# Batch 1's q and k by token blocks, a ring of six buffers and DMA transposes, in a sliding-window attention and MLP kernel

## The chip, the cores and the metric

The kernel runs on one core of a Trainium2 chip. The metric is the device time of one execution in microseconds (us). Before the change it is 224.65 us, the median of three runs (224.03 to 225.09). Engine names in the profile: PE is TensorE's matmuls, PEld its weight loads, DVE VectorE, ACT ScalarE, POOL GpSimd, SP SyncE, which only issues DMAs here. An ending q (SPq) marks an engine's queue of instructions. Runs are marked fast or slow by their own spread; ratios use fast runs alone.

## The reference, cut to what matters

```python
# q, k, v: (4, 8, 768, 64); n_sink 4, window 128; w_ch1 (512, 2048), w_ch2 (2048, 512)
keep = is_sink | ((rel >= 0) & (rel < 128))           # rel = query position - key position
scores = where(keep, q @ k.T / 8, -1e9)
a = exp(scores - max); a = a / sum(a)
x = (a @ v) as (batch, token, 512)
out = x + relu(layernorm(x) * g_ln @ w_ch1) @ w_ch2
```

The work is cut into 24 row blocks of 128 tokens, six in each of the four batches. Row blocks 6 to 11 are batch 1, 12 to 17 batch 2. Attention of one batch runs on TensorE between the MLP's products of earlier ones ("up" is the product with w1, "down" that with w2). The four sink tokens' scores are a product of their own, for queries 256 to 767.

## The kernel before

A list scheduler in Python walks all operations with estimated costs when the program is built, and so fixes the order in which each engine gets its instructions. In the traces each engine works through its own list in that order. This includes GpSimd and SyncE, which issue the DMAs: a load whose buffer isn't free holds up what stands behind it on that engine (at 86.05 us in the changed kernel's trace a load of q had waited 2.71 us for a transpose, and the six loads of v behind it were issued from 88.37).

```python
JOINED = (1, 3)
qkn = tile_pool(name="qkn", bufs=4)       # one buffer holds q or k of a whole batch
CHUNKS = {0: 2, 1: 1}                     # batches transposed on TensorE; the others by DMA
...
# masks of the attention weights: whichever engine the scheduler finds free
o = op({"POOL": 1.28, "DVE": 0.69}, window, [o, masks_done], key, (), [eb])
...
# batches 2 and 3: a load of 128 tokens, then a DMA transpose of it
def prep(b, x, r, lo, key):
    def go(_):
        nc.sync.dma_start_transpose(kb.t[:, x, :, 128 * r:128 * (r + 1)], qb.t[:, H * D * r:H * D * (r + 1)])
    o = op({"SP": 1.25}, go, [lo], key, alloc, [kb, qb])
...
for c in range(3):
    load_w(2, c, -440 + c)
for x in range(2):
    load_runs(1, 0, x, 0, H, 3.85, -436 + x)      # batch 1: q, then k, 768 KB each
load_w(2, 3, -434)
for r in range(RB):
    load_v(1, r, -430 + r)
load_first_v(1, -424)                              # the sink tokens' v
...
if b == 1:
    for hp in range(HP):
        prep_runs(1, 0, hp, k0 - 12 + 3 * hp)      # TensorE transposes
if b == 2:
    for r in range(RB):
        for x in range(2):
            load_qk(b, x, r, k0 - 60 + r)
    for r in range(RB):
        load_v(b, r, k0 - 50 + r, [prepped[(b, 3, 1)]])
```

The softmax here doesn't subtract the row's maximum and nothing guards it: scores larger than these inputs give would overflow.

## Time and profile before

| | before |
|---|---|
| median of the runs | 224.65 us |
| span of the profiled run | 222.8 us |
| TensorE busy | 215.7 us, 97% |
| share of TensorE in the chain that ended last | 89% |
| packets' time of the loads from GpSimd (q0), of the transposes and stores from SyncE (q1) | 71.6% and 24.8% of 16 engines' span |

TensorE is the bound: it has no idle of over 0.3 us between the start-up and the end. The DMA engines are full for the first half (nine tenths or more in slices 2 to 21 of the 40). The lines are quoted in the prediction. They are from GpSimd's timeline of the kernel before (start, duration, instruction, and in brackets the idle time before it with what ended it): the mask of batch 0's row block 5, and batch 2's six loads of v, issued as one block from 73.50 us.

```profile
33.09 1.09 POOL L642 TENSOR_SCALAR_AFFINE_SELECT e<-e 128x1024 bf16<-128x1024 bf16 x1 [1.11 <-ACT e L630]
...
73.50 5.36 POOL L418 DMA_DIRECT2D vn<-in_v_dram  x6
```

### The profile page before, as it was taken

To read this page: it belongs to the slowest core of one execution; us is meant where nothing else is said; L and a number is where in the kernel's file an instruction comes from. 1 tells how busy PE (TensorE), PEld (TensorE's weight loads), DVE (VectorE), ACT (ScalarE), POOL (GpSimd) and SP (SyncE) were. 2 spreads that over 40 slices of the span, in tenths; PEclk is the share of its full clock that TensorE was granted. 3 is DMA by queue.
4 is the path that set the end of the run, shared out by engine and by line. 5 is a ranking of instruction groups with operands and counts; after the bars stand their busy time and mean duration, and the time that the engine had idled before them with its cause. 6 is when DMAs were issued, how large, how long until landed. Compare 5 with 4: busy or idle time off the path is not lost.

```text
span 222.8 us, 4495 instructions
## 1 busy us (share of the span) xinstructions
PE 215.7 (97%) x1795; PEld 124.3 (56%) x1816; DVE 115.8 (52%) x246; ACT 111.1 (50%) x157; POOL 92.9 (42%) x129
## 2 busy tenths in 40 slices
PE   8999999999999999999999999999999999999994
PEld 7555888975465544455455445444454554444852
DVE  5447867036998898756763574570017660021011
ACT  3489785676761358861237753066603166400620
POOL 8996776449854986888500320120004020000000
PEclk9999999999999999999999999999999999999999
DMA  7999999999999999999993102311011220012102
GB/s 169 160 192 197 191 206 204 205 160 124 144 150 149 222 205 188 142 172 182 154 238 94 23 3 71 98 70 24 1 44 53 71 79 18 0 51 90 50 0 94
DMA packets 88582, 26.11 MB, mean 117 GB/s; under 512 B 78193, under 2 KB 85617, under 8 KB 88562
## 3 DMA queue, kind: packets, MB, share of 16 engines
q0 software_dynamic: 62656, 13.64, 71.6%
q1 hardware_dynamic: 25362, 11.81, 24.8%
q10 hardware_dynamic: 544, 0.39, 0.5%
q8 instruction: 14, 0.23, 0.4%
q14 instruction: 6, 0.05, 0.1%
HBM read 28.05 MB, written 6.29 MB: 154 GB/s over the span
## 4 chain that ended last, share of the span: by engine, by line
PE 89%; DVE 7%; issue 2%; ACT 1%; DVEq 0%; ACTq 0%
PE single L860 36%; PE single L820 35%; PE wide L612 4%; PE single L245 3%; PE single L697 2%; DVE st L749 2%; DVE xt L743 2%; DVE xn L757 2%; PE single L700 2%; PE wide L484 1%; PE wide L608 1%; PE single L680 1%; PE single L796 1%; PE single L484 1%; PE single L560 1%
## 5 line engine op out<-in xcount | busy, mean ns | idle before, releaser
L820 PE MATMUL single<-xnt,w1s 128*128 128x256 bf16 (+1 forms) x506 | 86.8, 325 | 0.3
L820 PEld LDWEIGHTS <-w1s 128*128 128x128 bf16 x512 | 48.8, 98 | 33.8 <-issue 2.1
L630 ACT ACTIVATE e<-wide 128x1024 bf16<-128x1024 f32 x44 | 43.8, 1022 | 47.6 <-PE wide L612 47.5
L860 PE MATMUL single<-w2s,h1t 128*128 128x512 bf16 x247 | 55.6, 379 | 1.0 <-issue 0.8
L873 DVE SCALAR_TENSOR_TENSOR ot<-single,rs,xt 128x512 f32<-128x512 f32 (+2 forms) x25 | 18.2, 728 | 55.5 <-PE single L860 55.0
L829 ACT ACTIVATE h1t<-single 128x512 bf16<-128x512 f32 x59 | 35.2, 597 | 21.3 <-PE single L820 19.8
L860 PEld LDWEIGHTS <-h1t 128*128 128x128 bf16 x256 | 24.6, 98 | 29.9 <-issue 0.9
L860 PE MATMUL single<-w2s,h1n 128*128 128x512 bf16 (+2 forms) x138 | 29.0, 355 | 0.5 <-issue 0.3
L642 POOL TENSOR_SCALAR_AFFINE_SELECT e<-e 128x512 bf16<-128x512 bf16 (+1 forms) x13 | 9.3, 713 | 47.5 <-ACT e L630 47.3
L829 ACT ACTIVATE h1n<-single 128x512 bf16<-128x512 f32 x30 | 17.9, 597 | 22.2 <-PE single L820 22.0
L418 POOL DMA_DIRECT2D vn<-in_v_dram x24 | 21.6, 910 | 0.3 <-DMA qkn<-in_k_dram 0.3
L757 DVE SCALAR_TENSOR_TENSOR xn<-xt,mv,gb 128x512 bf16<-128x512 bf16 x24 | 19.5, 814 | 0.9 <-DVE mv L752 0.3
L860 PEld LDWEIGHTS <-h1n 128*128 128x128 bf16 x144 | 12.7, 98 | 12.9 <-issue 1.1
L769 POOL TENSOR_SCALAR ve<-mv 128x2 f32<-128x2 f32 (+1 forms) x8 | 4.6, 570 | 29.3 <-DVE mv L752 29.1
L749 DVE BATCH_NORM_STATS2 st<-xt 128x6 f32<-128x512 bf16 x24 | 16.5, 688 | 0.3
L736 DVE RECIPROCAL rc<-single 128x4 f32<-128x4 f32 x34 | 6.0, 176 | 18.7 <-PE single L680 14.1
L737 DVE TENSOR_TENSOR xt<-single,rc 128x256 bf16<-128x256 f32 x34 | 14.4, 424 | 1.2
L697 PEld LDWEIGHTS <-e 128*128 128x128 bf16 x192 | 13.1, 98 | 2.5 <-issue 0.2
L612 PE MATMUL wide<-qkt 64*128 64x256 bf16 (+1 forms) x192 | 14.4, 262 | 0.0
L640 DVE TENSOR_TENSOR e<-e,mask 128x1024 bf16<-128x1024 bf16 x19 | 12.9, 686 | 2.4 <-ACT e L630 2.1
L409 POOL DMA_DIRECT2D qkn<-in_q_dram x12 | 11.0, 913 | 3.6 <-DMA vn<-in_v_dram 3.6
L700 PEld LDWEIGHTS <-e 128*128 128x128 bf16 x160 | 10.7, 97 | 1.7
(72 smaller groups left out, 186.0 us busy)
## 6 DMA issues: line engine op xcount, KB each, us to landing
out_dram<-ot SPq DMA_DIRECT2D x23, 256.0 KB, 2.0
vn<-in_v_dram POOLq DMA_DIRECT2D x24, 128.0 KB, 7.2
w1s<-in_moe_w_ch_dram POOLq DMA_DIRECT2D x4, 512.0 KB, 11.2
w2s<-in_moe_w_ch_dram POOLq DMA_DIRECT2D x4, 512.0 KB, 14.2
qkn<-in_q_dram POOLq DMA_DIRECT2D x12, 128.0 KB, 6.1
qkn<-in_k_dram POOLq DMA_DIRECT2D x12, 128.0 KB, 6.7
qkn<-in_q_dram POOLq DMA_DIRECT2D x1, 768.0 KB, 15.2
qkn<-in_k_dram POOLq DMA_DIRECT2D x1, 768.0 KB, 18.1
```

Source lines behind the costliest of these rows:

```text
L418: nc.gpsimd.dma_start(vn_buf[b % 2][:, r, :, 0:D], v[b, :, 128 * r:128 * (r + 1), :].rearrange("h p d -> p h d"))
L612: nc.tensor.matmul(pb.t[:, h2, i], lhsT=kb.t[64 * h2:64 * (h2 + 1), 1, hp, 128 * r:128 * (r + 1)], rhs=kb.t[64 * h2:64 * (h2 + 1), 0, hp, ...
L630: nc.scalar.activation(eb.t, pb.t, AF.Exp, scale=scale)
L697: nc.tensor.matmul(pv[:, hh, :], lhsT=weights_of(t, half, i, h2, 0), rhs=vn[:, r, h, 0:D + 1], start=fresh and hh == 0, stop=(r == 0), ski ...
L700: nc.tensor.matmul(pv[:, hh, :], lhsT=weights_of(t - 1, half, i, h2, 128), rhs=vn[:, r - 1, h, 0:D + 1], start=False, stop=not (joined and ...
L737: nc.vector.tensor_tensor(xb[t].t[:, 4 * half:4 * half + 4], pv[:, :, 0:D], rc[half].unsqueeze(2).to_broadcast([128, 4, D]), op=ALU.mult)
L749: nc.vector.bn_stats(st, xf)
L757: nc.vector.scalar_tensor_tensor(xnb[t].t, in0=xf, scalar=mvb[g][:, ti, 0:1], in1=gb, op0=ALU.subtract, op1=ALU.mult)
L820: nc.tensor.matmul(pb.t[:, n * i:n * (i + 1)], lhsT=w1s[:, j, 128 * (h0 + i):128 * (h0 + i + 1)], rhs=xtb[g].t[:, j, 0:n], start=(j == 0), ...
L829: nc.scalar.activation(hb.t, pb.t, AF.Relu)
L860: nc.tensor.matmul(pb.t[:, 0:n], lhsT=hidden(g, ht, ti), rhs=w2s[:, ht, c0:c1], start=(ht == 0), stop=(ht == NH1 - 1))
L873: nc.vector.scalar_tensor_tensor(ob.t[:, 0:n], in0=pb.t[:, 0:n], scalar=rsb[g][:, ti:ti + 1], in1=xb[t].t.rearrange("p h d -> p (h d)")[:, ...
```

## The change

The intent is to take batch 1's 96 transposes and the copies behind them off TensorE, ScalarE and VectorE, as batches 2 and 3 already do. All blocks of q and k of batches 1 to 3 now pass through six buffers of 128 KB. The scheduler now counts transposes (0.55 us each) and output stores as work of the DMA engines, as it did loads before.

```diff
-    JOINED = (1, 3)
+    JOINED = (3,)
+    QB = 6
-    qkn = ctx.enter_context(tc.tile_pool(name="qkn", bufs=4))
+    qkn = ctx.enter_context(tc.tile_pool(name="qkn", bufs=2))
+    qbp = ctx.enter_context(tc.tile_pool(name="qb", bufs=QB))
-    CHUNKS = {0: 2, 1: 1}
+    CHUNKS = {0: 2}
... (load_qk and prep: the block goes to a buffer qb of its own)
-        prepped[(b, r, x)] = op({"XD": 0.4}, None, [o], key, (), [kb, qb], 6.0)
+        prepped[(b, r, x)] = op({"DMA": 0.55}, None, [o], key, (), [kb, qb], 0.5)
... (sinks)
+        if b == 1:
+            part(256, 512, key, [eb])
+            part(512, S, akey(RB * b + 4) - 1, [])
+            return
+        return part(256, S, key, [eb])
... (masks)
-                    o = op({"POOL": 1.28, "DVE": 0.69}, window, [o, masks_done], key, (), [eb])
+                    engs = {"DVE": 0.69}
+                    if b != 1:
+                        engs["POOL"] = 1.28
+                    o = op(engs, window, [o, masks_done], key, (), [eb])
... (start-up: fewer warm-up products)
-                    n = int((min(s, 5.0) - f) / 0.107 + 0.9) if f < 5.0 else 0
-                    n += int((s - max(f, 5.0)) / 0.07 + 0.9) if s > 5.0 else 0
-                    n += 3 if s - f > 0.3 else 0
+                    n = int((s - f) / 0.107 + 0.9) + (3 if s < 5.0 else 0)
... (order of the loads)
-    for x in range(2):
-        load_runs(1, 0, x, 0, H, 3.85, -436 + x)
-    load_w(2, 3, -434)
+    load_first_v(1, -437)
+    load_qk(1, 0, 0, -436)
     for r in range(RB):
-        load_v(1, r, -430 + r)
-    load_first_v(1, -424)
+        if r < RB - 1:
+            load_qk(1, 0, r + 1, -436 + 2 * r)
+        load_qk(1, 1, r, -436 + 2 * r)
+        load_v(1, r, -435 + 2 * r)
+        if r == 1:
+            load_w(2, 3, -432.5)
... (prep_runs for batch 1 is gone)
```

More of the change, by code (lines that the diff above doesn't have):

```diff
@@ L135, in emit @@
                 s = max(r, free.get(e, 0.0))
-                cand.append((s, e, o, c))
+                cand.append((s, e, o, c, r))
                 first[e] = min(first.get(e, 1e9), s)
@@ L140, in emit @@
             lim = first[e0] + self.SLACK.get(e0, 0.0)
-            s, e, o, c = min((x for x in cand if x[1] == e0 and x[0] <= lim), key=lambda x: (x[2].key, x[0]))
-            if s < self.HOLD[0]:
-                s, e, o, c = min((x for x in cand if x[1] == e0 and (x[2] is o or x[2].key < o.key - 0.05 and
+            s, e, o, c, _ = min((x for x in cand if x[1] == e0 and x[0] <= lim),
+                                key=lambda x: (x[4] if e0 == "DMA" else 0.0, x[2].key, x[0]))
+            if s < self.HOLD[0] and e0 != "DMA":
+                s, e, o, c, _ = min((x for x in cand if x[1] == e0 and (x[2] is o or x[2].key < o.key - 0.05 and
                                   x[0] < min(s + c - 0.12, s + self.HOLD[1]))), key=lambda x: (x[2].key, x[0]))
@@ L356, in qn_buf @@
             return []
-        qn[(b, x)] = Buf("qkn", 4)
+        qn[(b, x)] = Buf("qkn", 2)
         return [qn[(b, x)]]
@@ L401, in load_qk @@
     def load_qk(b, x, r, key, deps=()):
-        alloc = qn_buf(b, x)
-        qb = qn[(b, x)]
+        qb = Buf("qb", QB)
         def go(_):
-            if qb.t is None:
-                qb.t = qkn.tile([128, H * S * D // 128], BF16, name="qkn")
-            dst = qb.t.rearrange("p (r h d) -> p r h d", r=RB, h=H)
-            nc.gpsimd.dma_start(dst[:, r], (q, k)[x][b, :, 128 * r:128 * (r + 1), :].rearrange("h p d -> p h d"))
-        o = load(0.9, 0.9, go, key, deps, alloc, [qb])
-        prep(b, x, r, o, key)
+            qb.t = qbp.tile([128, H * D], BF16, name="qb")
+            nc.gpsimd.dma_start(qb.t.rearrange("p (h d) -> p h d", h=H),
+                                (q, k)[x][b, :, 128 * r:128 * (r + 1), :].rearrange("h p d -> p h d"))
+        prep(b, x, r, load(0.9, 0.9, go, key, deps, [qb]), key, qb)
     vcast, vread, vs_done = {}, {}, {}
@@ L450, in go @@
                                     bass.AP(src.tensor, src.offset, [[0, 128 // NS]] + list(src.ap)))
-        first_in[b] = op({"XD": 0.1}, None, [load(3.4, 0.9, go, key, deps, [fb])], key, (), [fb], 0.0 if b == 1 else 8.0)
+        first_in[b] = op({"XD": 0.1}, None, [load(3.4, 0.9, go, key, deps, [fb])], key, (), [fb], 0.0 if b == 1 else 3.0)
     prepped, kqb, turns = {}, {}, {}
@@ L498, in prep_runs, with prep @@
                 prepped[(b, c, hp, x)] = o
-    def prep(b, x, r, lo, key):
+    def prep(b, x, r, lo, key, qb):
         alloc = qkt_buf(b)
-        kb, qb = kqb[b], qn[(b, x)]
+        kb = kqb[b]
         def go(_):
@@ L507, in go @@
                 kb.t = qkt.tile([128, 2, HP, S], BF16, name="qkt")
-            nc.sync.dma_start_transpose(kb.t[:, x, :, 128 * r:128 * (r + 1)], qb.t[:, H * D * r:H * D * (r + 1)])
+            nc.sync.dma_start_transpose(kb.t[:, x, :, 128 * r:128 * (r + 1)], qb.t)
         o = op({"SP": 1.25}, go, [lo], key, alloc, [kb, qb])
-        prepped[(b, r, x)] = op({"XD": 0.4}, None, [o], key, (), [kb, qb], 6.0)
+        prepped[(b, r, x)] = op({"DMA": 0.55}, None, [o], key, (), [kb, qb], 0.5)
     def ready(b, hps, klo, khi, qlo, qhi):
@@ L528, in sinks @@
         kb = kqb[b]
-        pb, eb = Buf("pm", 0), Buf("es", 2)
+        eb = Buf("es", 2)
         esb[b] = eb
@@ L555, in pick_v @@
                                     smask.unsqueeze(2).to_broadcast([128, H, D]), op=ALU.mult)
-        def mm(_):
-            pb.t = room_for(pb)
-            for hp in range(HP):
-                nc.tensor.matmul(pb.t[32 * hp:32 * (hp + 1), :], lhsT=ks[:, hp, :], rhs=kb.t[:, 0, hp, 256:S],
-                                 start=True, stop=True, skip_group_check=True)
-        def ex(_):
-            eb.t = espool.tile([128, S - 256], BF16, name="es")
-            nc.scalar.activation(eb.t, pb.t, AF.Exp, scale=scale)
-        o1 = op({"DVE": 0.2}, mul_k, ready(b, range(HP), 0, NS, 0, 0) + [sunk.get(b - 2), sinks_done, edone.get((RB * b, 0)) if b else None], key, (), [kb])
+        o1 = op({"DVE": 0.2}, mul_k, ready(b, range(HP), 0, NS, 0, 0) + [sunk.get((b - 2, r)) for r in range(2, RB)] + [sinks_done, edone.get((RB * b, 0)) if b else None], key, (), [kb])
         if b == 0:
@@ L572, in sinks, with part, mm, ex @@
             vs_done[b] = op({"DVE": 0.6}, pick_v, [first_in[b], sinks_done, vread.get((b - 2, RB - 1))], key, (), [first_v[b]])
-        deps = [o1] + ready(b, range(HP), 0, 0, 256, S)
-        def rest(o2):
-            sunk[b] = op({"ACT": 0.6}, ex, [o2], key, [eb], [pb])
-        if joined:
-            return Joined(mm, deps, [pb], [kb], 0.32, rest)
-        rest(op({"PE": 0.4}, mm, deps, key, [pb], [kb]))
+        def part(q0, q1, key, alloc):
+            pb = Buf("pm", 0)
+            def mm(_):
+                pb.t = room_for(pb)
+                for hp in range(HP):
+                    nc.tensor.matmul(pb.t[32 * hp:32 * (hp + 1), 0:q1 - q0], lhsT=ks[:, hp, :], rhs=kb.t[:, 0, hp, q0:q1],
+                                     start=True, stop=True, skip_group_check=True)
+            def ex(_):
+                if eb.t is None:
+                    eb.t = espool.tile([128, S - 256], BF16, name="es")
+                nc.scalar.activation(eb.t[:, q0 - 256:q1 - 256], pb.t[:, 0:q1 - q0], AF.Exp, scale=scale)
+            def rest(o):
+                o = op({"ACT": 0.2 + 0.0008 * (q1 - q0)}, ex, [o], key, alloc, [pb] + ([] if alloc else [eb]))
+                for r in range(q0 // 128, q1 // 128):
+                    sunk[(b, r)] = o
+            deps = [o1] + ready(b, range(HP), 0, 0, q0, q1) + ([] if alloc else [sunk[(b, 2)]])
+            if joined:
+                return Joined(mm, deps, [pb], [kb], 0.11 + 0.0004 * (q1 - q0), rest)
+            rest(op({"PE": 0.2 + 0.0004 * (q1 - q0)}, mm, deps, key, [pb], [kb]))
+        if b == 1:
[3 more added lines that the diff above has]
+        return part(256, S, key, [eb])
     ebuf = {}
@@ L714, in values @@
         if r >= 2:
-            deps += [sunk[b], vs_done[b]]
+            deps += [sunk[(b, r)], vs_done[b]]
             uses += [esb[b]]
@@ L787, in normalise @@
                    [xnb[t], xtb[g]])
-            turned[t] = op({"XD": 0.4}, None, [o], key, (), [xnb[t], xtb[g]], 8.0 if t < 10 else 6.0 if t < 18 else 0.0)
+            turned[t] = op({"DMA": 0.55}, None, [o], key, (), [xnb[t], xtb[g]], 0.5)
             return
@@ L880, in down @@
             o = op({"DVE": 0.17 + 0.58 * n / 512}, fin, [o, rs_done[g]], key - 20, [ob], [pb, xb[t]])
-            op({"SP": 0.7}, put, [o], -300 + key, (), [ob])
+            o = op({"SP": 0.7}, put, [o], -300 + key, (), [ob])
+            op({"DMA": 0.65}, None, [o], key, (), [ob])
     pre_down = {}
@@ L914 @@
         for x in range(2):
-            load_runs(0, 1, x, 4 * half, 4 * half + 4, ((1.1, 1.0), (1.05, 2.1))[half][x], -498 + 2 * half + x)
+            load_runs(0, 1, x, 4 * half, 4 * half + 4, ((2.0, 1.05), (1.0, 1.1))[half][x], -498 + 2 * half + x)
         if half == 0:
@@ L919 @@
     for c in range(4):
-        load_w(1, c, -470 + 2 * c, 2.6 if c else 2.25)
+        load_w(1, c, -470 + 2 * c, 2.6 if c else 2.5)
         load_v(0, 2 + c, -469 + 2 * c)
@@ L956 @@
             continue
-        if b == 1:
-            for hp in range(HP):
-                prep_runs(1, 0, hp, k0 - 12 + 3 * hp)
         if b == 2:
```

## The prediction

> **What bounds the kernel now.** I read the page's busy shares first, then the chain of work that ended last, then TensorE's timeline where the changed transposes sit, then the DMA lines.
>
> ```profile
> span 222.8 us, 4495 instructions
> PE 215.7 (97%) x1795; PEld 124.3 (56%) x1816; DVE 115.8 (52%) x246; ACT 111.1 (50%) x157; POOL 92.9 (42%) x129
> PE   8999999999999999999999999999999999999994
> DMA  7999999999999999999993102311011220012102
> GB/s 169 160 192 197 191 206 204 205 160 124 144 150 149 222 205 188 142 172 182 154 238 94 23 3 71 98 70 24 1 44 53 71 79 18 0 51 90 50 0 94
> PE 89%; DVE 7%; issue 2%; ACT 1%; DVEq 0%; ACTq 0%
> ```
>
> TensorE has almost no gap from 20 us to the end, and the chain is TensorE for 89%. The DMA engines are also full, but only for the first 21 slices of 5.6 us. So work taken off TensorE shortens the kernel, if the full DMA of the first half still delivers in time. The timeline of TensorE from 45 to 52 us (start, duration, group):
>
> ```profile
> 45.65 1.53 PE L484 MATMUL wide<-ident,qkn 128*64 128x128 bf16 x48
> 47.11 1.05 PE L820 MATMUL single<-xnt,w1s 128*128 128x256 bf16 x8
> 48.39 1.73 PE L484 MATMUL wide<-ident,qkn 128*64 128x128 bf16 x48 [0.23 <-DVE qkt L233]
> 50.05 1.92 PE L820 MATMUL single<-xnt,w1s 128*128 128x256 bf16 x16
> ```
>
> The two x48 groups are batch 1's q and k transposes (L484). From 45.65 to 47.11 and from 48.16 (the end of the up products) to 50.05 they take 1.46 + 1.89 = 3.35 us, the 0.23 us wait included.
>
> What replaces them is seen in batch 2, which already goes by loads of 128 tokens and DMA transposes. The DMA issues between 49.5 and 59.6 us (count, size, median us from issue to landing), and the POOL queue's two big batch-1 loads and the SP queue's first batch-2 transposes in the timelines:
>
> ```profile
> qkn<-in_q_dram POOLq DMA_DIRECT2D x6, 128.0 KB, 6.3
> qkn<-in_k_dram POOLq DMA_DIRECT2D x6, 128.0 KB, 7.3
> qkt<-qkn SPq DMA_TRANSPOSE x4, 7.1
> ...
> 24.99 0.91 POOL L369 DMA_DIRECT2D qkn<-in_q_dram  x1
> 25.89 0.89 POOL L369 DMA_DIRECT2D qkn<-in_k_dram  x1
> ...
> 53.47 5.42 SPq L508 DMA_TRANSPOSE qkt<-qkn  x4
> ```
>
> A transpose takes some 1.3 us of SP to issue and lands 6 to 9 us after its issue while loads are queued; later, with fewer loads, 4.1 to 5.
>
> [...] a TensorE transpose shows 219 ns and is pipelined to 32 ns apart (1.53/48), a DMA transpose of 128x512 lands after 6 us and more. [...] batch 2's first loads land every 1.0 us (53.40, 54.39, 55.41); beside transposes the next land at 56.92, 58.90, 60.73 and the transposes at 59.4, 61.8, 63.4. [...] from 53.47 to 65.1, 8 loads and some 4.6 transposes in 11.6 us; with 0.9 us a load, 0.95 us a transpose.
>
> **The change, part by part.**
>
> (a) *Removed:* 96 TensorE transposes and the wait, 3.35 us on the path. Also 4 ScalarE copies of 0.80 us and 4 VectorE copies of 0.95 us, not on the path beyond the 0.23 already counted.
>
> (b) *Sinks in two parts:* eight products of 256 columns for four of 512 (the four took 0.33 us). The columns are the same; estimate +0.1 us TensorE. One more ScalarE exponential, hidden.
>
> (c) *Masks of batch 1 all on VectorE:* POOL did four of them (63.4 to 68.8). Four times 0.69 = 2.8 us more for VectorE between 55 and 70, where the before shows
>
> ```profile
> 50.10:77.30 27.20, 26.78 (x255) 15.21 (x260) 23.23 (x51) 14.26 (x17) 20.37 (x27) 1.00 1.80 159
> ```
>
> (the third figure after the length, 23.23, is VectorE). Copies of 1.8 us leave this stretch and 2.8 come in: 24.2 of about 27 us. I walked VectorE's new order with its measured durations (normalising 1.2, statistics and centring 1.6, mask 0.64, output 0.7): the masks of row blocks 3 and 4 end about 1.3 and 1.8 us before TensorE's value products want them. Tight, free.
>
> (d) *Start-up:* six fewer warm-up products before the second group of batch-0 transposes. They are on the chain (12 products, 5.72 to 7.11), while the casts that the transposes need end at 5.87. Six at 0.116 us = 0.7 us earlier[...]. This is worth something only if nothing later waits for DMA.
>
> (e) *The new DMA path.* TensorE's new order after the up products: 12 downs, scores 6, 12 downs, scores 7, values 6, first sinks part. Ups end at 51.97 - 3.35 = 48.6. A down is 0.216 us (2.59 for 12), scores 0.55, values 0.30. So scores 6 are due at 51.2, scores 7 at 54.35, the first sinks part at 55.2 (54.6 with the start-up gain). They need the transposes of q0,q1,k0; q2,k1; q3.
>
> The DMA order is now: w2's third quarter (landed at 36.25 before, nothing ahead of it changes), four first-row loads of v (1.0 us), q0, q1, k0, v0, q2, k1, v1, w2's last quarter (2.5 us: 43.99 to 46.51 before), q3. So q0 lands at about 38.2. From there until q3: q1, k0, v0, q2, k1, v1, q3 at 0.88 = 6.2, w2 2.5, and the five transposes already under way at 0.95 = 4.75. Sum 13.4: q3 lands at 51.5. Issue does not limit it: [...] POOL issues q3 near 42. Its transpose then takes 4.1 to 6 us: 55.6 to 57.5, centre 56.4. The first sinks part was due at 54.6: TensorE waits 1.8 us there (1.2 of 55.2 if the start-up gains nothing).
>
> The others by the same count: q0,q1,k0 land transposed at 44 to 48 (due 51.2), q2,k1 at 49.5 to 51.5 (due 54.35), k2 at about 59 (scores 8 due at 58 plus the wait, 59.3), q4,k3 at 62 to 63 (due 64), q5,k4 at 65 to 67 (due 67). k2 and later loads wait for a free ring buffer, so for the transposes of q0, q1, k0 and so on; with six buffers they run some 9 us behind, and the margins above are about 1 us. Batch 2's loads start near 60, when the ring lets them, rather than at 49.7; its first scores are due near 79.
>
> *Sum:* span 222.8 - 3.35 + 0.1 = 219.55 with the sinks due at 55.2, so the end is 164.35 us after their start. Started at 56.4: 220.75. The timed runs are 1.85 us over the span (224.65 - 222.8): **222.6 us**.
>
> **Rivals.**
> 1. *The whole gain.* The transposes land in time because their latency is nearer to 4 us and the loads run at 0.85 us (as v's between w1's quarters, 17.63 to 18.47). For: the sinks were split, which lets the first part do without q4, q5, and the loads are ordered by need. Against: 6 us and more in the only stretch with loads beside transposes. End 218.9 to 219.5, time 220.8 to 221.4, with all small gaps closed 220.2.
> 2. *The ring is too small.* Each reuse waits for load, transpose and issue; scores 8, 9, 10 stop one after another, and SP, which issues in order, is held by an output store between transposes. For: margins of 1 us, store waits of up to 14 us in SP's before. Against: the third blocks are already 9 us later than the first. Another 2 to 3 us: 225.
> 3. *VectorE becomes the bound* in 55 to 78 us. For: busy 9 tenths there already. Against: walk (c), and any TensorE wait for q3 gives it slack. At most 1 us.
> 4. *The gain was hidden anyway*, because ups wait for w1 or downs for w2: against, the 40.0 to 45.6 us stretch has TensorE busy 5.60 of 5.60, and w2's third quarter lands 12 us before use. Its last is now wanted at 51.75, and lands near 50.5: close, but before q3's transpose.
>
> **Range and chances.** The q3 landing is uncertain by 2 us either way, start-up by 0.6, later stops by 0 to 2. So 220.3 to 225.0. Faster than 2% means under 220.2: all of (a), the start-up gain and no wait: 8%. Slower than 2% means over 229.1, which needs 9 us of new waits: 2%.
>
> **What would show it.** (a) No x48 groups of transposes; ups end at 48 to 48.7 and run unbroken into downs. (e) An idle of 1 to 3 us on TensorE before the first sinks product near 55, ended by a DMA transpose of the ring buffer; transposes landing 5 to 7 us after issue near 50; POOL waiting for transposes before its ring loads. (c) VectorE over 9 tenths between 55 and 78, TensorE not waiting for it over 0.5 us in sum. (d) First up product at 20.5 in place of 21.2. The prediction is wrong if TensorE waits at scores 6 or 7 (loads later than counted), at scores 8 to 10 over 1 us each (ring), or nowhere (latency overestimated).

## The result

The changed kernel takes 234.68 us (median of four runs, 234.13 to 237.14; a fifth took 233.31) against 224.87 us for the kernel before in the same rounds (224.03 to 226.53). The ratio is 1.0405, with a 95% interval of 1.0335 to 1.0476: slower. A ratio here is the mean time of one kernel's fast runs over that of the other's fast runs of the same rounds, so it is not quite the ratio of the medians that are quoted.

The page of the changed kernel (span, busy times, busy tenths in 40 slices, TensorE's granted clock in tenths, the DMA engines in tenths, and the chain that ended last by engine):

```profile
span 235.1 us, 4369 instructions
...
PE 217.1 (92%) x1716; PEld 121.8 (52%) x1716; DVE 113.2 (48%) x246; ACT 109.3 (47%) x156; POOL 93.1 (40%) x127
...
PE   8989993999699998299998999999999999999994
...
PEclk9999998899999999769999999999999999999998
DMA  7999999999999999999999960232001321012102
...
PE 62%; DMA 24%; POOL 7%; DVE 3%; issue 2%; SPq 1%; ACT 0%; DVEq 0%; POOLq 0%
```

TensorE's work is nearly the same, 217.1 us, but its share fell to 92%. Two stretches show where: near 39 us and near 97 us its clock falls, and beside them its busy share. The DMA row is full to slice 23 in place of 21. In the chain, DMA and GpSimd now hold 31%, which had not been in it before.

This profile is of a slow run (237.14 us). A second, below, shows the same waits at the same places, but it is of a slow run too (236.98 us). The fast runs recorded the same mean clock (0.975 to 0.985), and profiles of fast runs of kernels below, in which one or the other wait was left alone, show these waits: 4.34 us at 39 us (experiments 3 and 10), 2.77 and 3.46 us in batch 2 (experiment 2).

TensorE's waits (what waited, and what ended it: us in sum, times, longest):

```profile
PE single L570 <- DMA qkt<-qb: 5.8, 2, 4.0
PE wide L713 <- POOL e L655: 4.3, 1, 4.3
PE single L713 <- DMA vn<-in_v_dram: 1.4, 1, 1.4
...
PE single L713 <- POOL e L655: 1.0, 1, 1.0
```

L713 and L716 are the value products, L570 the sinks' scores. The five waits sum to 12.4 us. TensorE's timeline gives their places, by the start of the product that waited: 39.30 us (4.29, row block 5 of batch 0), 61.73 (1.81, first sinks of batch 1), 94.72 (1.38, batch 2's v), 99.63 (3.96, sinks of batch 2) and 125.81 (0.96).

```profile
39.30 0.23 PE L713 MATMUL wide<-vn,e 128*128 128x65 bf16 x1 [4.29 <-POOL e L655]
...
61.73 0.29 PE L570 MATMUL single<-qkt,ks 128*32 128x256 bf16 x4 [1.81 <-DMA qkt<-qb]
```

```profile
94.72 0.42 PE L713 MATMUL single<-vn,e 128*128 128x65 bf16 x8 [1.38 <-DMA vn<-in_v_dram]
...
99.63 0.62 PE L570 MATMUL single<-qkt,ks 128*32 128x512 bf16 x4 [3.96 <-DMA qkt<-qb]
```

The first wait has nothing to do with batch 1's transposes. GpSimd's timeline in the same run, where the mask (L655) of row block 5 stands behind loads:

```profile
35.14 0.88 POOL L409 DMA_DIRECT2D qb<-in_k_dram  x1 [2.24 <-DMA w2s<-in_moe_w_ch_dram]
36.10 0.22 POOL L785 TENSOR_SCALAR ve<-mv 128x2 f32<-128x2 f32 x1
36.40 0.72 POOL L787 TENSOR_TENSOR rs<-ve,neg_half 128x2 f32<-128x2 f32 x1
37.18 0.94 POOL L418 DMA_DIRECT2D vn<-in_v_dram  x1
38.14 1.11 POOL L655 TENSOR_SCALAR_AFFINE_SELECT e<-e 128x1024 bf16<-128x1024 bf16 x1
```

A load of k waited 2.24 us until a quarter of w2 had landed; behind it came two small steps of the layernorm and a load of v, and only then the mask. In the kernel before the same mask ran at 33.09 us. (In both traces no load from GpSimd is issued while more than seven earlier ones have not landed; this one went out at 35.14 us, when the eighth before it, the quarter of w2, had landed at 34.33.)

The last lines of interest are GpSimd's loads for batch 2:

```profile
86.05 0.87 POOL L409 DMA_DIRECT2D qb<-in_q_dram  x1 [2.71 <-DMA qkt<-qb]
87.51 0.87 POOL L409 DMA_DIRECT2D qb<-in_k_dram  x1 [0.58 <-DMA qkt<-qb]
88.37 5.26 POOL L418 DMA_DIRECT2D vn<-in_v_dram  x6
```

Batch 2's v is issued from 88.37 us, 14.9 us later than before. It stands behind all twelve loads of q and k, and those wait for ring buffers: GpSimd waited for DMA transposes 13 times, 26.9 us in sum, where the kernel before had no such wait.

**The sum.** In the profiled pair the span grew by 12.3 us. The waits give 12.4. The clock is at half from 39.17 to 42.58 us and from 97.19 to 104.02, of which TensorE still waited until 39.30 and 99.63; half of the remaining 3.3 and 4.4 us, 3.8 in sum, is lost (an estimate). TensorE's removed work gives back 3.35 and the start-up 0.86. That makes 12.0, against 12.3 seen. The first down product starts 0.6 us later than before (53.03 against 52.45); but before, row block 6's scores (0.55 us) were already done by then and now they are not, so at equal work the lag is 1.1 us. By then the gains had paid for most of the first wait; the first sinks' wait follows, and most of the rest is lost between 91 and 135 us, in batch 2.

### The profile page after: what moved, and what is told of

It reads as the page before. It is cut to its first block, busy times and chain, and to the rows that moved or that the text cites.

```text
span 235.1 us, 4369 instructions
## 1 busy us (share of the span) xinstructions
PE 217.1 (92%) x1716; PEld 121.8 (52%) x1716; DVE 113.2 (48%) x246; ACT 109.3 (47%) x156; POOL 93.1 (40%) x127
## 4 chain that ended last, share of the span: by engine, by line
PE 62%; DMA 24%; POOL 7%; DVE 3%; issue 2%; SPq 1%; ACT 0%; DVEq 0%; POOLq 0%
PE single L876 29%; PE single L836 26%; DMA qkt<-qb 9%; DMA w2s<-in_moe_w_ch_dram 6%; DMA qb<-in_q_dram 6%; DMA vn<-in_v_dram 3%; PE wide L625 2%; POOL qb L409 1%; PE single L713 1%; POOL qkn L371 1%; PE single L716 1%; POOL vn L418 1%; POOL rs L787 1%; PE single L696 1%; POOL e L655 1%
## 5 line engine op out<-in xcount | busy, mean ns | idle before, releaser
L836 PE MATMUL single<-xnt,w1s 128*128 128x256 bf16 (+1 forms) x512 | 89.3, 333 | 0.0
L836 PEld LDWEIGHTS <-w1s 128*128 128x128 bf16 x512 | 50.0, 100 | 35.8 <-issue 4.4
L876 PE MATMUL single<-w2s,h1t 128*128 128x512 bf16 x256 | 57.0, 379 | 0.0
L889 DVE SCALAR_TENSOR_TENSOR ot<-single,rs,xt 128x512 f32<-128x512 f32 (+2 forms) x25 | 18.2, 728 | 66.3 <-PE single L876 65.5
L409 POOL DMA_DIRECT2D qb<-in_q_dram x18 | 16.1, 892 | 18.2 <-DMA qkt<-qb 13.7
L409 POOL DMA_DIRECT2D qb<-in_k_dram x18 | 16.0, 890 | 17.1 <-DMA qkt<-qb 13.3
L655 POOL TENSOR_SCALAR_AFFINE_SELECT e<-e 128x512 bf16<-128x512 bf16 (+1 forms) x7 | 4.9, 705 | 39.2 <-ACT e L643 39.2
L653 DVE TENSOR_TENSOR e<-e,mask 128x1024 bf16<-128x1024 bf16 x25 | 16.7, 682 | 4.9 <-ACT e L643 4.7
L773 DVE SCALAR_TENSOR_TENSOR xn<-xt,mv,gb 128x512 bf16<-128x512 bf16 x24 | 18.2, 758 | 0.6
L713 PEld LDWEIGHTS <-e 128*128 128x128 bf16 x192 | 13.2, 99 | 10.2 <-POOL e L655 6.0
L625 PE MATMUL wide<-qkt 64*128 64x256 bf16 (+1 forms) x192 | 14.4, 262 | 0.0
L713 PE MATMUL single<-vn,e 128*128 128x65 bf16 x136 | 10.1, 193 | 2.3 <-DMA vn<-in_v_dram 1.4
```

The lines of the kernel that those rows point to most:

```text
L409: nc.gpsimd.dma_start(qb.t.rearrange("p (h d) -> p h d", h=H), (q, k)[x][b, :, 128 * r:128 * (r + 1), :].rearrange("h p d -> p h d"))
L625: nc.tensor.matmul(pb.t[:, h2, i], lhsT=kb.t[64 * h2:64 * (h2 + 1), 1, hp, 128 * r:128 * (r + 1)], rhs=kb.t[64 * h2:64 * (h2 + 1), 0, hp, ...
L653: nc.vector.tensor_tensor(ev, ev, mask1[:, 0:n].unsqueeze(1).to_broadcast([128, m, n]), op=ALU.mult)
L713: nc.tensor.matmul(pv[:, hh, :], lhsT=weights_of(t, half, i, h2, 0), rhs=vn[:, r, h, 0:D + 1], start=fresh and hh == 0, stop=(r == 0), ski ...
L773: nc.vector.scalar_tensor_tensor(xnb[t].t, in0=xf, scalar=mvb[g][:, ti, 0:1], in1=gb, op0=ALU.subtract, op1=ALU.mult)
L836: nc.tensor.matmul(pb.t[:, n * i:n * (i + 1)], lhsT=w1s[:, j, 128 * (h0 + i):128 * (h0 + i + 1)], rhs=xtb[g].t[:, j, 0:n], start=(j == 0), ...
```

## The experiments

In each diff, minus is the changed kernel unless another is named. They ran in four groups, and each group has its own runs of the kernel before, whose median is given with each result. In 2, 3, 4, 8 and 12 the order of everything else stays. In 5, 6 and 9 to 11 the scheduler plans anew, so that from some point on more than the edit differs from the kernel that each starts from (GpSimd's list from 24 us in 6, from 62 in 9, from 64 in 10). In 2, 3, 4, 6 and 9 to 12 the measured time lies outside the ranges of both theory and rival, by under 0.6 us in 2, 6 and 11 and by about 1 us or more in the others.

### 1. The changed kernel again

No edit.

> The changed kernel unchanged, for a profile in the fast state. If the waits seen in the first profile are its own and not of the slow state: TensorE waits of 4.3 us near 39 (mask on POOL), 1.5 to 4 us at the first sinks part, 1 to 3 us for batch 2's v near 95, 3.5 to 4.5 us at batch 2's sinks near 99, 1 us near 126; time 233.3 to 235. If not, one of them is missing and the time of its fast runs is explained by the others.

Measured: 234.04 us (233.36 to 236.98), before 225.67, ratio 1.038. TensorE's waits are 4.17 us at 38.96, 1.20 at 60.90, 1.14 at 93.64, 4.16 at 98.75 and 0.97 at 125.65. The result and its places repeat; single waits vary by some tenths of a us.

### 2. Row block 5's mask on VectorE

```diff
-                if e == "DVE":
+                if e == "DVE" or t == 5:
```

The order of everything else is the same.

> Instruction order as in the changed kernel, except that the mask of batch 0's last row block goes from POOL to VectorE. In the changed kernel TensorE waits 4.3 us for that mask at 35 to 39.3 us. Theory A (the DMA path binds: q3's transpose lands at 61.7 whatever TensorE does before): the 4.3 us wait vanishes, TensorE comes to the first sinks part near 55.5 and waits 5 to 6.5 us there for q3's transpose, which lands between 60 and 62; time 233 to 234.7. Rival B (the waits add up): the wait for q3 stays near 1.8 us, its landing moves earlier with TensorE; time 227.5 to 229.5, i.e. 4.3 us of wait and 1.5 us of half clock less.

Measured: 234.88 us (233.74 to 236.28), before 224.69, ratio 1.0435. The wait at 39 us is gone, and nothing is gained. TensorE's timeline:

```profile
54.42 0.42 PE L713 MATMUL single<-vn,e 128*128 128x65 bf16 x8
58.94 0.41 PE L570 MATMUL single<-qkt,ks 128*32 128x256 bf16 x4 [4.10 <-DMA qkt<-qb]
```

The first sinks' wait is 4.10 us in place of 1.81: the first wait had only hidden it. This run is also the cleanest test of the prediction's step (e). With GpSimd free, the last value product before the sinks ends at 54.84 us (54.6 predicted), q3 lands at 52.49 (51.5 predicted), and its transpose lands 6.4 us after issue, at 58.9 (56.4 predicted). Batch 2's waits stay, 2.77 and 3.46 us.

### 3. Twelve buffers in the ring

```diff
-    qbp = ctx.enter_context(tc.tile_pool(name="qb", bufs=QB))
+    qbp = ctx.enter_context(tc.tile_pool(name="qb", bufs=12))
```

The scheduler still counts six, so that every engine's order is unchanged; only the waits for buffers go.

> Instruction order exactly that of the changed kernel; only the ring has twelve buffers in place of six, so a load waits for the transpose twelve blocks before. Theory A (the ring of six delays batch 2's blocks, and with them the second batch's sinks (4.0 us of wait, 2.2 us lost to half clock) and its v (1.4 us)): those waits vanish, POOL no longer waits 27 us for transposes; the mask wait of 4.3 us and the first sinks wait stay (1.8 us, perhaps up to 4 since more loads compete); time 226 to 229. Rival B (the DMA engines themselves are the limit, not the ring): batch 2's transposes land no more than 2 us earlier, waits of 3 us or more stay near 97 us; time 232 to 235.

Measured: 236.41 us (235.99 to 236.78), before 224.69, ratio 1.0494: slower still. The first sinks' wait grows to 3.34 us, that of batch 2 is 3.22, and only the wait for batch 2's v shrinks (0.46). Beside loads that start earlier, the transpose of q3, for which TensorE waits, took 6.88 us to land, against 5.57 in the changed kernel. The ring's reuse is not what costs the time in batch 1.

### 4. Both of these

> Both edits. Theory A (the first wait only hides a later one): 0 to 1.5 us better than the twelve buffers alone, 225 to 228, with a wait of 5 to 8 us for q3's transpose at the first sinks part. Rival B (waits add): 220 to 222.5, the predicted gain after all.

Measured: 233.91 us (231.95 to 234.3), before 224.69, ratio 1.0372. Two waits are left, both for transposes before sinks: 4.55 us in batch 1 and 4.49 us in batch 2. Neither cure reaches them.

### 5. Batch 1 back on TensorE, the rest of the change kept

```diff
-    CHUNKS = {0: 2}
+    CHUNKS = {0: 2, 1: 1}
-    load_first_v(1, -437)
-    load_qk(1, 0, 0, -436)
+    for x in range(2):
+        load_runs(1, 0, x, 0, H, 3.85, -436 + x)
+    load_w(2, 3, -434)
... (v's blocks and the sinks' v as before; three whole-batch buffers; prep_runs for batch 1)
```

> The changed kernel with batch 1's q and k loaded in two big transfers and transposed on TensorE as before; the other parts of the change kept (fewer warm-up products, batch 1's masks on VectorE, sinks of batch 1 in two parts, ring of six for batches 2 and 3). Theory A (all of the loss comes from batch 1's new DMA path, the rest is harmless): the before less the start-up gain of 0.8 us: 223.5 to 225. Rival B (the masks on VectorE or the ring in batches 2 and 3 cost by themselves): TensorE waits of 1 us or more near 60 to 100 us; 226 or more.

Measured: 229.01 us (227.56 to 231.91, the last of these slow), before 224.69, ratio 1.015 with an interval of 1.0076 to 1.0224, so unclear at 2%. Thus 1.5% of the 4.05% remain without a single DMA transpose in batch 1 (by the interval, between a fifth and a half of the loss). After the start-up and up to 95 us TensorE has no wait over 0.7 us. Then a value product of batch 2 waits 1.97 us for a mask on GpSimd, which stands behind a load that waited 1.54 us for a ring buffer, and 3.4 us at half clock follow (the run's mean clock is 0.992). So the new loads of q and k cost time in batch 2 as well. That it is the ring alone is not shown: the scheduler's new estimates are kept here too, and in experiment 11, with the same ring and another order of loads, the wait is gone.

### 6. w2's last quarter right behind the others, and row block 5's mask on VectorE

```diff
-    for c in range(3):
-        load_w(2, c, -440 + c)
+    for c in range(4):
+        load_w(2, c, -441 + c)
...
-        if r == 1:
-            load_w(2, 3, -432.5)
```

> The kernel with the row block's mask on VectorE, and w2's last quarter loaded right behind the other three, ahead of all of batch 1. In the run with the mask alone q3 landed at 52.5, its transpose at 58.9, and TensorE waited 4.1 us for it. Theory A (a transpose is slow above all beside w2's large packets: from 47.1 to 52.5 in the changed kernel the engines did a w2 quarter, 2.5 us alone, and about one transpose): the transposes of q2 and k1 land by 51 and 53 or sooner, q3's at 55.5 to 57, TensorE waits under 2 us; time 231.5 to 233.5. Rival B (a transpose costs the DMA engines the same 1.4 us or so beside any load, so order changes nothing): q3's transpose lands at 58.5 to 60, wait 3.5 to 5 us; time 234 to 236.

Measured: 231.18 us (229.87 to 233.44, the last slow), before 225.67, ratio 1.0244 (1.0174 to 1.0315, so unclear at 2%). Against experiment 2 the ratio fell by 0.019, some 4 us. The waits in its profile (a slow run):

```profile
PE single L713 <- DMA vn<-in_v_dram: 3.8, 1, 3.8
PE single L570 <- DVE xn L773: 3.1, 1, 3.1
...
PE single L570 <- DMA qkt<-qb: 0.8, 1, 0.8
...
PE wide L625 <- DMA qkt<-qb: 0.5, 1, 0.5
```

Batch 1's sinks now wait 0.8 us and its scores (L625) 0.5. The transpose of q3 lands at 55.91, 3.0 us earlier than in experiment 2: 2.0 of this because q3 itself lands earlier (50.53), 1.0 because the transpose takes 5.36 us. Batch 2's v (3.8) and sinks (3.1) are what is left. The releaser named for the latter is VectorE's xn, which the sinks do not read. A DMA transpose of q or k issued at 89.37 us landed at 97.28, 0.24 us before the sinks ran, so I take this wait too for one on transposes.

### 7. DMA alone

A kernel of its own that gives a wrong result (zeros). It times transfers in separate phases: eight loads of 128 tokens; eight transposes of 128x512; both together; two quarters of w1 (512 KB each); those with six transposes; one load of 768 KB; that with eight transposes. A column of each landed tile is read by VectorE before the next phase starts.

> A kernel with a wrong result (zeros) on purpose, which measures the disputed cost by itself. In turn, each after the one before has landed: 8 block loads of 128 KB; 8 transposes of 128x512; 8 of both at once; two w1 quarters; two w1 quarters with 6 transposes; one load of 768 KB in long runs; the same with 8 transposes. If a transpose costs what the prediction took (0.95 us of the DMA engines): both at once, from first to last landing, 8 x (0.9 + 0.95) = 15 us at most, less the overlap of their latencies; two quarters with six transposes 5 + 5.7 = 11 us. If it costs 1.4 us: 18 and 13.5 us. If large packets crowd it out: beside w1 the transposes land late, with the w1 quarters or after them, and the sum is over 14 us. Block loads alone 0.85 to 0.95 us apart, the long load 3.9 us.

Measured, from the trace of its one run (112.72 us). The landing times of the transposes (issue to landing, us: least, median, most) are in three phases alone, beside block loads, and beside weights:

```profile
DMA to landing us min/median/max: 2.5/2.5/2.5
```

```profile
DMA to landing us min/median/max: 5.2/7.2/8.0
```

```profile
DMA to landing us min/median/max: 2.4/6.8/8.4
```

Alone they land in 2.5 us. Beside block loads the median is 7.2; beside weights all but the first, which ran before the weights moved, take 5.3 to 8.4. (Beside the 768 KB load they take 2.4 to 7.4.) The work that they add is much smaller. Eight loads alone take 10.46 us from first issue to last landing; with eight transposes 16.64: 0.77 us for each transpose. Two weight quarters alone take 8.0 us; with the transposes 11.8, and as five of the six fell in that time this is 0.76 each.

These differences would be too small if the DMA engines had idled in the phases without transposes. But alone, too, the packets of the eight take only 43.1% of the engines' time over 12 us (14 to 26), 0.65 us each. So a transpose costs the DMA engines less than the 0.95 us that the prediction used, beside weights too, and my own theory from the changed kernel's landings, that it costs some three times as much there, falls. What grows is the time until one of them has landed, from 2.5 us to a median of 7.2 and 6.8.

### 8. The kernel before with only the new warm-up rule

The diff (minus is the kernel before) is the three lines on n in the change above.

> The kernel before with only the rule for the warm-up products changed (six fewer before the second group of batch 0's transposes). Theory A (they are on the chain at the start, and TensorE is the bound from 20 us on): 0.7 to 0.9 us faster, 223.8 to 224.1 against 224.7 (ratio 0.996 to 0.997). Rival B (the start-up gain is lost in a later wait for DMA): no difference beyond 0.2 us.

Measured: 225.47 us (224.55 to 227.43, six runs), before 225.67, ratio 1.0023 with an interval of 0.9969 to 1.0077: the same. The first up product starts at 20.36 us in place of 21.17, and 0.69 us of this are kept until 117 us. There they are lost in one wait:

```profile
PE single L818 <- DVE ot L871: 0.8, 1, 0.8
```

VectorE was late because it had waited 2.53 us for an output store to free its buffer; SyncE issued the stores of that stretch some 2 us later than before. So the start-up gain is real, and in this profile it is lost again. The times cannot tell: their interval, from 0.7 us faster to 1.7 slower, holds both outcomes.

### 9. Batch 2's loads reordered and its sinks in two parts, in experiment 6's kernel

```diff
                 for x in range(2):
                     load_qk(b, x, r, k0 - 60 + r)
-            for r in range(RB):
-                load_v(b, r, k0 - 50 + r, [prepped[(b, 3, 1)]])
+                load_v(b, r, k0 - 60 + r)
...
-        if b == 1:
+        if b in (1, 2):
             part(256, 512, key, [eb])
```

> The kernel with w2's last quarter early and row block 5's mask on VectorE, and in addition batch 2's v loads between its q and k loads (they waited behind all twelve of them) and batch 2's sinks' scores in two parts too. Theory A: the two waits of TensorE that were left in it, 3.79 us for batch 2's v and 3.12 us for batch 2's sinks, go, and with them the two stretches of 3.4 us at half clock that followed them (up to 1.7 us each): 231.2 - 6.9 - 2 to 3.4 = 221 to 222.5 us, so below the kernel before. Rival B: the waits only move, because v now takes the slots in GpSimd's queue from q and k and the DMA engines are as busy as they were: 227 to 231, with the wait at the sinks over 3 us.

Measured: 224.59 us (223.06 to 227.34, the last slow), before 224.72, ratio 0.9978 (0.9931 to 1.0026): level with the kernel before. The wait for batch 2's v is gone. Of batch 2's sinks 2.13 us remain in the profiled run, which is the slow one, and half clock behind it (0.91 in the mean from 80 to 100 us); the fast runs recorded a mean clock of 0.997 to 1.0, so this half clock is hardly in them. Five waits for transposes are left in that profile, 4.5 us in sum:

```profile
PE single L570 <- DMA qkt<-qb: 2.9, 2, 2.1
PE wide L625 <- DMA qkt<-qb: 1.6, 3, 0.6
```

### 10. The same two edits, in the changed kernel itself

> The changed kernel with only the two edits for batch 2 (v between q and k, sinks in two parts). Theory A: its waits for batch 2 (1.4 and 4.0 us) and the 6.8 us at half clock that followed (up to 3.4 us) go, those near 39 us (4.3) and 62 us (1.8) stay: 234.2 - 5.4 - 2 to 3.4 = 225.5 to 227 us. Rival B: 232 to 235.

Measured: 227.96 us (227.09 to 228.92), before 224.72, ratio 1.0133. The two edits take away some 6 us (234.68 and 234.04 to 227.96). Batch 2's waits shrink from 5.34 to 0.5 us, and no half clock is left behind them (the profile's mean clock is 0.992, against 0.975); the wait of 4.34 us at 39 us stays. In the profile two other waits are smaller as well: the first sinks' is 0.41 us, though every engine's order is the same up to there, and that of 0.96 us near 126 us is gone. The theory expected 225.5 to 227: the direction is right, the size 1 us short.

### 11. The same two edits, with batch 1 on TensorE

The edits of 9 in the kernel of 5.

> The kernel with batch 1 back on TensorE, with the two edits for batch 2 alone. Theory A: its one wait of 1.97 us and the 3.4 us at half clock behind it go: 229.0 - 2.0 - 1 to 1.7 = 225.3 to 226 us, level with the kernel before; then the kernel with DMA transposes for batch 1 and all queues mended is 2.5 to 4 us below it, which is what batch 1's TensorE transposes cost (3.35 us). Rival B: stays at 228 to 229, and the difference to the first kernel of this call is under 1 us.

Measured: 224.74 us (224.04 to 228.45, the last slow), before 224.72, ratio 0.9991. After the start-up no wait over 0.65 us and no half clock remain (mean clock 1.0). As expected it is level with the kernel before. What failed is the second half of the expectation: experiment 9's kernel, the same but for batch 1's DMA transposes and what they need, is not 2.5 to 4 us faster but equal (224.59). In the profiles it is 3.6 us ahead when both have done 192 up and 12 down products and row block 6's scores (50.56 against 54.15), about the size of the removed transposes; 0.9 us ahead at 204 up and 96 down products (82.24 against 83.15); and 2.8 us behind from 97 us on. Its waits for DMA transposes take the lead away; the last step is that of its slow profiled run, with 2.13 us of wait and the half clock behind it.

### 12. Experiment 9's kernel with twelve buffers

The edit of 3 in the kernel of 9; the engines' orders are the same.

> The kernel with w2 early, row block 5's mask on VectorE and both edits for batch 2, with twelve ring buffers in place of six and every engine's order as it was. In it GpSimd still waited 27.1 us for ring buffers, and TensorE waited for transposes five times, 4.5 us in sum, with 3.4 us at half clock behind the longest (2.13 us). Theory A (with the queues mended the ring is now what holds back q and k): at least 3 of the 4.5 us and the half clock go, 220.5 to 222.5 us, below the kernel before. Rival B (DMA engines, not buffers: earlier loads only slow the transposes of batch 1): 223.5 to 226, the first sinks' wait over 2 us.

Measured: 227.34 us (227.12 to 228.54), before 224.85, ratio 1.0115. Batch 2's waits are gone, as buffers would have it, but batch 1's have grown:

```profile
54.22 0.61 PE L625 MATMUL wide<-qkt 64*128 64x256 bf16 x8 [1.41 <-DMA qkt<-qb]
...
57.20 0.40 PE L570 MATMUL single<-qkt,ks 128*32 128x256 bf16 x4 [2.02 <-DMA qkt<-qb]
```

The first scores wait 1.41 us, the sinks 2.02, and 6.8 us at half clock follow (the mean clock from 53 to 63 us is 0.66). This is experiment 3's effect again: loads that run ahead slow the transposes which are needed first. The transpose of q3 was issued at 49.74 us in experiment 9 and at 49.72 here, and landed after 4.25 us there and 7.44 here. The six buffers of the change do hold the loads back to some purpose. No kernel beats the kernel before by more than the runs' spread.

## Why the prediction was wrong

**Step (a), right.** The x48 groups of transposes are gone and TensorE's transposes with them. The gain is real: experiment 9 is 3.6 us ahead of experiment 11 at 50 us.

**Steps (b) and (c), right.** The sinks' products take 0.2 us more in the trace (0.1 estimated). After the start-up TensorE waits for VectorE 0.12 us, on one tile of the layernorm, and for no mask of batch 1. VectorE was busy 17.1 us between 50.1 and 77.3, not the 24.2 foreseen: its blocks came later, so there was more room than counted.

**Step (d), right on the start, wrong on the end.** The first up product came at 20.31 us (20.5 predicted), but the profile of experiment 8 shows that in the kernel before the same gain is lost again at one wait.

**Step (e), right in the order and the load count, wrong in the rest.** That "the margins above are about 1 us" was not what failed first. Nor did any of the three signs of being wrong come true: scores 6 to 10 of batch 1 do not wait. The wait at the first sinks, 1.81 us where 1.8 was predicted, is luck: TensorE came there at 59.92 us and not at 54.6, and the transpose landed at 61.69 and not at 56.4. Three terms failed:

1. *The transpose's time to land.* "Its transpose then takes 4.1 to 6 us": 6.4 us in experiment 2, where q3 itself landed within 1 us of the count. The prediction had read "6 to 9 us after its issue while loads are queued" from the trace, and then took the shorter time for a stretch with loads queued. In the changed kernel q3 landed at 56.10 and the transpose at 61.69. Experiment 7 shows that the DMA work of a transpose is no larger than was counted (0.77 us against 0.95); the landing time is what traffic beside it stretches (2.5 us alone, 7.2 in the median beside block loads). w2's last quarter, which the change put between q2 and q3, was in the way: with it moved ahead (6), and the plan made anew behind it, the kernel is some 4 us faster.
2. *A queue that was never walked.* The prediction followed VectorE's order and TensorE's, not GpSimd's. There batch 0's last mask stood behind two loads, and TensorE waited 4.29 us. "Issue does not limit it" was true of q3 (issued at 42.55, 42 predicted) and blind to what stood between the loads. Experiment 2 shows both that this was the cause and that curing it alone gains nothing, as the wait behind it comes out.
3. *The end of the sum.* "the end is 164.35 us after their start" took all that follows the first sinks as fixed. It was noted that batch 2's loads start near 60 us, but only its first scores were checked. Its v came 14.9 us later and its sinks waited. In experiment 10 two edits to batch 2, with the plan made anew from there on, take away some 6 of the 10 us, and experiment 5 loses time in batch 2 even without DMA transposes in batch 1.

A fourth term was in no step: the clock. In the changed kernel's trace it is at half for 3.41 us from 39.17 us and for 6.83 us from 97.19, and both stretches begin inside TensorE's long waits (35.01 to 39.30 and 95.67 to 99.63); in the trace of the kernel before it is at 1.00 from 5 to 222 us. By an estimate from these, a long wait cost up to 1.7 us more for each 3.41 us at half clock. Which waits were followed by half clock is in the last section.

**The rivals.** Rival 1 fell with the landing times. Rival 2, the ring, was right in part and for batch 2 only: twelve buffers end batch 2's waits in 12 but leave 3.22 us of them in 3, and they make batch 1 worse in both. Rival 3 did not happen. Rival 4 named w2's last quarter as close; it landed at 52.53 us (50.5 foreseen), but the harm was to q3 behind it and to the transposes beside it.

**What stays open.** Between 47 and 53 us the DMA engines moved 115 GB/s in the changed kernel and 108 in its second look, but 163 in experiment 2, whose loads up to q3 are issued within 0.8 us of the same times. Here q3 lands 3.6 us later in the changed kernel than in experiment 2; no run tests why. The traces show that most of the shortfall lies in two or three microseconds that end in a near stop: 85, 104 and 12 GB/s from 49 to 52 us, 50 and 13 from 49 to 51 in the second look, and never under 146 in a whole microsecond of experiment 2's stretch. Before the stop, at 50.13 and 48.96 us, a fetch of instructions (16 KB, queue q8) starts; in experiment 2 no such fetch falls there (40.40 and 62.56). Other fetches are followed by such stops too (that at 64.75 by 6 GB/s between 65.5 and 66.5), but not all (that at 32.28 is not), so this is a hint and not a cause. Untested as well is what the scheduler assumes of a transpose: by its constants it is ready 8.45 us after its issue begins in the kernel before, and after 4.4 us plus the wait for its turn among the DMA work in the changed one, where those of batch 1 took 3.6 to 11.2. The two edits of experiment 9 were not run apart, so the share of each is not known.

## What to carry to other kernels

When work goes from a busy engine to DMA, count not only the transfers' work but how long one of them takes to land among the others (a transpose here 2.5 us alone, 7.2 in the median beside block loads), and order the big transfers that nobody needs yet out of their way (some 4 us in experiment 6). Walk every in-order queue that issues transfers for what stands between them, a mask as much as a load (here one behind a load that waited 2.24 us), and follow the last transfer through to the next batch. A wait that is removed may only uncover the next one (4.10 us in place of 1.81 in experiment 2), so judge by the end, not by the wait.

## What the traces show of landings and of the clock

- DMA transposes: as work, 0.76 to 0.77 us were added for each in experiment 7, where a block load's step was 0.87. The landing time, which is what a kernel waits for, was 2.5 us alone, 7.2 in the median beside block loads, and up to 8.4 beside weights.
- TensorE's waits and its clock: waits of 1.97 us (experiment 5) and 2.13 us (the slow run of 9) were each followed by 3.4 us at half clock, while one of 1.81 us (first sinks, changed kernel) was not: the clock there is 1.00 from 42.58 to 97.19 us. In the changed kernel the half clock with the wait of 4.29 us lasted 3.41 us, that with the wait of 3.96 us 6.83. In experiment 12 waits of 1.41 and 2.02 us, 1 us apart, went with 6.8 us of it. What decides whether half clock follows, and for how long, no run tested.
